# The last 128 tokens' second product in two halves of 256 columns, the second stored from ScalarE's queue

## The chip, the cores and the metric

One core of one Trainium2 chip. The metric is the device time of one execution of the program in microseconds; the median of three runs is compared. A profiled execution gives the span from the first to the last instruction and, for every engine, what it ran, what it waited for and which transfers it started.

## The reference

Eight batches of eight heads, 576 positions, head size 64. Attention looks back over a window of 64 positions; its output, laid out as 4608 tokens of 512 values, goes through two products with a hard-swish between them:

```python
scores = scale * np.matmul(q, k.transpose(0, 1, 3, 2))
mask = (rel >= 0) & (rel < window)
scores = np.where(mask, scores, -1000000000.0)
attn = softmax(scores)                       # written out in the reference
x = np.matmul(attn, v).transpose(0, 2, 1, 3).reshape(B * S, H * D)   # 4608 x 512
h = x @ w_in                                 # 512 -> 2048
g = h * np.clip(h + 3.0, 0.0, 6.0) / 6.0
out = (g @ w_out).astype(np.float32)         # 2048 -> 512
```

## The kernel before

Everything is written out by hand; no scheduler moves an instruction. An attention part makes the tokens, transposed, into `xT`. The two products run over nine blocks of 512 tokens. For each block, `first_units` (line 495) gives 16 units, one for each 128 of the 2048 hidden values: four matmuls into a bank `hT` (line 513), ScalarE's ReLU (line 525), VectorE's product (line 526) into `gT`. `second_units` (line 534) gives 16 more: four for each of the block's four groups of 128 tokens (`ts`), each unit with four matmuls of 128x512 (line 550), so that 16 of them sum up one bank `acc`. Behind the fourth unit of a group, ScalarE copies the bank into `osb` (line 556) and SP issues its store of 256 KB to `out` (line 558). `osb` comes from a pool of three buffers, `acc` of the last group of the last block from the pool `ps_t` of three banks.

The units stand in a list, `moe`, that the attention part draws from (`weave`, line 600) while it goes on. `queue_block` (line 567) puts a block's first units and second units of the block before into it. At the end, `queue_last` (line 581) appends block 7's remaining second units among block 8's first units, and then block 8's second units, four groups in order. So the last thing that TensorE does is the 16 matmuls of block 8's group `ts` = 3, and the last things at all are their copy and their store.

Ahead of that, `flagged` (line 605) tests whether all sums of the softmax were in range, each engine loads the flag (line 936), and behind the last unit stands a branch (line 938): if the flag is clear, `general` computes everything again in a safe way. Here it never is, so every engine jumps over the code of the fallback, which on each engine stands between the last unit and the program's end. Behind the jump each engine waits for its own instructions, SP also for the counters of all hardware DMA queues, eight of them (both under line 938); then SP reads further counters and the engines meet at GpSimd, which clears the semaphores (line 965).

ScalarE issues no DMA in this kernel: stores and SBUF-to-SBUF copies and transposes are issued by SP, loads by GpSimd.

Of the kernel before, what the change touches and what calls it, by code (L numbers as in the profile page):

```python
# [10 lines left out]
F32 = mybir.dt.float32  # L11
# [14 lines left out]
P = 128  # L26
# [11 lines left out]
def kernel(  # L38
# [9 lines left out]
    nc = tc.nc  # L48
    B, H, S, _ = q.shape
    DM, FF = moe_w_in.shape  # L50
# [5 lines left out]
    NFC = FF // P  # L56
    TB = 512
    XR = 6 * TB
    NTB = NT // TB
# [9 lines left out]
    osbp = ctx.enter_context(tc.tile_pool(name="osb", bufs=3))  # L69
    ps_o = ctx.enter_context(tc.tile_pool(name="ps_o", bufs=1, space=PSUM))  # L70
    ps_t = ctx.enter_context(tc.tile_pool(name="ps_t", bufs=3, space=PSUM))
# [11 lines left out]
    wout16 = consts.tile([P, NFC, DM], BF16, name="wout16")  # L83
# [409 lines left out]
    halfway, units, firsts = {}, {}, {}  # L493
# [40 lines left out]
    def second_units(kb):  # L534
        gT = gTs[kb]
        units, both = [], []
        for ts in range(TB // P):
            state = {}

            def unit(i, ts=ts, state=state):  # L540
                if i == 0 and late[0] == 0 and ts in (1, 2):
                    if ts == 1:
                        both.append(ps_o.tile([P, 2, 512], F32, name="acco", tag="o"))
                    state["acc"] = both[0][:, ts - 1]
                elif i == 0:
                    pool = ps_t if ts == 1 or late[0] == 2 and ts == 3 else ps_acc
                    state["acc"] = pool.tile([P, DM], F32, name="acc", tag="bk")[:]
                acc = state["acc"]
                for fc in range(4 * i, 4 * i + 4):
                    nc.tensor.matmul(  # L550
                        acc, lhsT=gT[:, fc, ts * P : (ts + 1) * P], rhs=wout16[:, fc, :],
                        start=(fc == 0), stop=(fc == NFC - 1),
                    )
                if i == NFC // 4 - 1:
                    osb = osbp.tile([P, DM], F32, name="osb")
                    nc.scalar.copy(out=osb[:], in_=acc)  # L556
                    u0 = kb * TB + ts * P
                    nc.sync.dma_start(out=out[u0 : u0 + P, :], in_=osb[:])

            units += [lambda i=i, unit=unit: unit(i) for i in range(NFC // 4)]  # L560
        return units

    moe = deque()
# [3 lines left out]
    def queue_block(kb, kept=2 * NG, lead=2):  # L567

        f = first_units(kb)
        moe.extend(left[:lead])  # L570
        del left[:lead]
        n = len(left)
        for i, unit in enumerate(f):
            moe.extend(left[i * n // NFC : (i + 1) * n // NFC])
            moe.append(unit)
        left[:] = second_units(kb)
        n = len(left) - kept
        moe.extend(left[:n])
        del left[:n]
# [109 lines left out]
    def warm(pool, n, cols=TB):  # L689
# [12 lines left out]
        out=ident[:], in_=ident[:], pattern=[[-1, P]], compare_op=mybir.AluOpType.not_equal,  # L702
# [115 lines left out]
    n = NG  # L818
# [151 lines left out]
```

## Time and profile before

| | us |
|---|---|
| runs | 315.24, 315.67, 315.19; median 315.24 |
| profiled execution | 316.28 |
| its span, first to last instruction | 314.6 |
| TensorE busy | 299.5 (95%) |
| ScalarE busy | 184.6 (59%) |
| VectorE busy | 180.4 (57%) |
| GpSimd busy | 131.3 (42%) |
| last copy of `acc` | 308.45 to 309.03 |

In the profile PE is TensorE's matmuls, PEld its weight loads, ACT ScalarE, DVE VectorE, POOL GpSimd and SP SyncE; an engine's name with a q (SPq, ACTq, PEldq) stands for its queue of issuing, branch and semaphore instructions, which aren't counted as busy. A row of a source line gives the count, the shortest, median and longest duration in ns, and the first and last start in us from the span's start. Timeline rows give start, length, and what ran. Groups give busy us and mean ns of one behind the bar, then the idle time before them and what ended it. "DMA to landing" is the time from a store's issue until its semaphore has its full count.

### The profile page before, as it was taken

The page shows a single profiled execution, that of the slowest core. Times are in us where ns is not written, and L with a number is a line of the kernel's source. Part 1 is how long each engine was busy: PE and PEld are TensorE (multiplying, and loading weights), DVE is VectorE, ACT ScalarE, POOL GpSimd, SP SyncE. Part 2 cuts the span into 40 slices and gives each one's busy share as a digit, 9 for nine tenths or more (in the row PEclk, how much of TensorE's full clock was granted, in tenths as well). Part 3 has the DMA queues.
Part 4 walks back from the last instruction along what each step waited for, and adds up shares of the span by engine and source line. Part 5 has one row for each costly group of instructions (what it writes and reads, how often), then busy time and mean ns, then how long its engine had stood idle before and what let it go on. Part 6 is the DMA issues. An engine that isn't in the chain of part 4 may idle for free.

```text
span 314.6 us, 10707 instructions
## 1 busy us (share of the span) xinstructions
PE 299.5 (95%) x4565; PEld 151.0 (48%) x4608; DVE 180.4 (57%) x411; ACT 184.6 (59%) x350; POOL 131.3 (42%) x181
## 2 busy tenths in 40 slices
PE   7889989999999999999999999999999999999992
PEld 3454445555555554444555555555544444444440
DVE  7767647598547755773577447754776155344200
ACT  3838555877658656773677457754764266454410
POOL 8861404868887536653665366533330000000000
PEclk9999999999999999999999999999999999999998
DMA  8999995969996976697469744983021100100121
GB/s 155 167 205 200 198 192 123 220 119 100 205 144 102 144 167 114 76 132 188 84 83 139 169 109 79 131 193 88 19 56 52 69 33 0 70 34 33 36 82 60
DMA packets 57848, 35.96 MB, mean 114 GB/s; under 512 B 40128, under 2 KB 51904, under 8 KB 57792
## 3 DMA queue, kind: packets, MB, share of 16 engines
q0 software_dynamic: 35744, 18.52, 45.8%
q1 hardware_dynamic: 22048, 16.67, 21.0%
q8 instruction: 38, 0.62, 0.8%
q14 instruction: 18, 0.15, 0.1%
HBM read 37.62 MB, written 9.44 MB: 150 GB/s over the span
## 4 chain that ended last, share of the span: by engine, by line
PE 81%; DMA 9%; POOL 3%; DVE 3%; issue 2%; ACT 1%; POOLq 0%; ACTq 0%; DVEq 0%
PE acc L550 36%; PE hT L513 34%; DMA qk<-in_q_dram 7%; PE o L421 4%; PE s L323 3%; DMA V<-in_v_dram 2%; PE tk L289 2%; PE acco L550 1%; POOL qk L117 1%; PE tq L289 1%; DVE gT L526 1%; POOL qk L128 1%; POOL wout L179 1%; DVE opl L448 0%; DVE V L160 0%
## 5 line engine op out<-in xcount | busy, mean ns | idle before, releaser
L526 DVE SCALAR_TENSOR_TENSOR gT<-t,hT 128x512 bf16<-128x512 bf16 x141 | 95.7, 686 | 74.3 <-ACT t L525 73.2
L513 PE MATMUL hT<-xT,win 128*128 128x512 bf16 x548 | 131.5, 379 | 1.1 <-DVE gT L526 0.2
L550 PE MATMUL acc<-wout,gT 128*128 128x512 bf16 x522 | 126.7, 379 | 2.5 <-issue 1.1
L525 ACT ACTIVATE t<-hT,half_const 128x512 bf16<-128x512 f32 x141 | 95.6, 689 | 48.2 <-PE hT L513 46.3
L513 PEld LDWEIGHTS <-win 128*128 128x128 bf16 x576 | 55.3, 98 | 65.2 <-issue 0.4
L550 PEld LDWEIGHTS <-gT 128*128 128x128 bf16 x576 | 54.5, 98 | 64.2 <-issue 0.9
L344 POOL TENSOR_TENSOR Pz<-e,band 128x512 bf16<-128x512 bf16 x48 | 54.1, 1144 | 0.0
L341 POOL TENSOR_TENSOR P<-e,first 64x256 bf16<-64x256 bf16 x24 | 15.8, 660 | 74.4 <-ACT e L332 74.4
L556 ACT COPY osb<-acc 128x512 f32<-128x512 f32 x34 | 19.9, 586 | 42.0 <-PE acc L550 42.0
L336 ACT ACTIVATE e<-s 128x512 bf16<-128x512 f32 x56 | 30.1, 591 | 0.0
L296 DVE COPY KT<-tk 128x576 bf16<-128x576 bf16 x28 | 21.0, 749 | 6.9 <-ACT e L332 5.8
L147 POOL DMA_DIRECT2D V<-in_v_dram x22 | 18.0, 829 | 8.5 <-DMA wout<-in_moe_w_out_dram 5.6
L448 DVE TENSOR_TENSOR opl<-o,recs 128x256 bf16<-128x256 f32 x52 | 19.6, 419 | 0.5
L430 DVE TENSOR_REDUCE sums<-o 128x10 f32<-128x20 f32 x26 | 4.6, 175 | 23.9 <-PE o L421 23.8
L296 ACT COPY QT<-tq 128x576 bf16<-128x576 bf16 x27 | 17.2, 638 | 1.5 <-PE tq L289 1.5
L332 ACT ACTIVATE e<-tk 64x128 bf16<-64x128 f32 x28 | 7.6, 270 | 17.7 <-PE tq L309 17.7
L421 PEld LDWEIGHTS <-Pz 64*64 64x64 bf16 x1008 | 11.4, 108 | 10.7 <-issue 10.2
L289 PE MATMUL tk<-ident,qk 64*64 64x64 bf16 x504 | 14.3, 195 | 0.0
L289 PE MATMUL tq<-ident,qk 64*64 64x64 bf16 x504 | 14.0, 195 | 0.3 <-DMA qk<-in_q_dram 0.3
L128 POOL DMA_DIRECT2D qk<-in_k_dram x22 | 14.1, 640 | 0.3 <-issue 0.3
L323 PE MATMUL s<-QT,KT 64*64 64x64 bf16 x896 | 13.8, 194 | 0.0
L128 POOL DMA_DIRECT2D qk<-in_q_dram x22 | 13.8, 627 | 0.0
(106 smaller groups left out, 199.9 us busy)
## 6 DMA issues: line engine op xcount, KB each, us to landing
out_dram<-osb SPq DMA_DIRECT2D x36, 256.0 KB, 2.5
V<-in_v_dram POOLq DMA_DIRECT2D x16, 256.0 KB, 6.0
qk<-in_q_dram POOLq DMA_DIRECT2D x19, 144.0 KB, 4.5
qk<-in_k_dram POOLq DMA_DIRECT2D x19, 144.0 KB, 4.3
V<-V SPq DMA_DIRECT2D x6, 432.0 KB, 5.1
wout<-in_moe_w_out_dram POOLq DMA_DIRECT2D x2, 1024.0 KB, 17.4
qk<-in_k_dram POOLq DMA_DIRECT2D x6, 288.0 KB, 4.4
qk<-in_q_dram POOLq DMA_DIRECT2D x6, 288.0 KB, 5.6
```

The lines of the kernel that those rows point to most:

```text
L128: nc.gpsimd.dma_start(out=t[halves[z], hs], in_=src[b, hs].rearrange("h (p r) d -> p h (r d)", r=RL))
L289: nc.tensor.transpose(out=hosts[t][z][halves[h], r * W : (r + 1) * W], in_=staged[b][halves[z], 2 * g + h, r * D : (r + 1) * D], identity= ...
L296: (nc.scalar.copy if z and not on_vector else nc.vector.tensor_copy)(out=(QT[t % 4][:] if z else KT[t % 4][:, W:]).rearrange("q (p r) -> q ...
L323: nc.tensor.matmul(ss[h][halves[i], c, m, r], lhsT=keys(t, h, W * (w - 1), r), rhs=QT[t % 4][halves[h], w * W : (w + 1) * W], start=True, ...
L336: nc.scalar.activation(out=e[:].rearrange("p c m r w -> p (c m r w)"), in_=ss[h][:].rearrange("p c m r w -> p (c m r w)"), func=EXP, scale ...
L344: muls[h].tensor_tensor(out=Pw[t % 4][:, h].rearrange("p c m r w -> p (c m) (r w)"), in0=e[:].rearrange("p c m r w -> p (c m) (r w)"), in1 ...
L421: nc.tensor.matmul(o[i][halves[c], c0 : c0 + D + 1], lhsT=p, rhs=vt[:, hh, v0 : v0 + D + 1], start=(r == 0), stop=(r == 1), skip_group_che ...
L513: nc.tensor.matmul(hT, lhsT=win16[:, g, fc * P : (fc + 1) * P], rhs=xT[:, g, t0 : t0 + TB], start=(g == 0), stop=(g == NG - 1),)
L525: nc.scalar.activation(out=t1[:], in_=hT, func=RELU, bias=half_const[:], scale=1.0 / 6.0)
L526: nc.vector.scalar_tensor_tensor(out=gT[:, fc, :], in0=t1[:], scalar=1.0, in1=hT, op0=MIN, op1=MULT)
L550: nc.tensor.matmul(acc, lhsT=gT[:, fc, ts * P : (ts + 1) * P], rhs=wout16[:, fc, :], start=(fc == 0), stop=(fc == NFC - 1),)
L556: nc.scalar.copy(out=osb[:], in_=acc)
```

## The change

In the last group of the last block (`kb` = 8, `ts` = 3), and in the same group of the fallback, the units are replaced by `half_unit`. The first two units make columns 0 to 255 with eight matmuls of 128x256 each, the last two columns 256 to 511. Each half has a bank of `ps_t`, a copy by ScalarE into a buffer of the same three `osb` buffers, and a store of 128 KB. The first half's store is issued by SP, the second half's by ScalarE. The `tag` only keeps the two shapes in one pool of three. The counters that SP waits for behind the jump are the same eight; ScalarE's store counts in one of them.

```diff
-                    osb = osbp.tile([P, DM], F32, name="osb")
+                    osb = osbp.tile([P, DM], F32, name="osb", tag="osb")
                     nc.scalar.copy(out=osb[:], in_=acc)
                     u0 = kb * TB + ts * P
                     nc.sync.dma_start(out=out[u0 : u0 + P, :], in_=osb[:])
 
-            units += [lambda i=i, unit=unit: unit(i) for i in range(NFC // 4)]
+            def half_unit(i, ts=ts, state=state):
+
+                j, part = divmod(i, 2)
+                n = DM // 2
+                cols = slice(j * n, (j + 1) * n)
+                if part == 0:
+                    state[j] = ps_t.tile([P, n], F32, name="acc", tag="bk")
+                for fc in range(8 * part, 8 * part + 8):
+                    nc.tensor.matmul(
+                        state[j][:], lhsT=gT[:, fc, ts * P : (ts + 1) * P], rhs=wout16[:, fc, cols],
+                        start=(fc == 0), stop=(fc == NFC - 1),
+                    )
+                if part:
+                    osb = osbp.tile([P, n], F32, name="osbh", tag="osb")
+                    nc.scalar.copy(out=osb[:], in_=state[j][:])
+                    u0 = kb * TB + ts * P
+                    (nc.scalar if j else nc.sync).dma_start(out=out[u0 : u0 + P, cols], in_=osb[:])
+
+            last = kb == NTB - 1 and ts == TB // P - 1
+            units += [lambda i=i, unit=half_unit if last else unit: unit(i) for i in range(NFC // 4)]
         return units
```

## The prediction

> **What bounds the kernel now.** I read the page first, then the timeline of the last 20 us, then the rows of the branch and closing lines.
>
> ```profile
> span 314.6 us, 10707 instructions
> ...
> PE 299.5 (95%) x4565; PEld 151.0 (48%) x4608; DVE 180.4 (57%) x411; ACT 184.6 (59%) x350; POOL 131.3 (42%) x181
> ...
> PE 81%; DMA 9%; POOL 3%; DVE 3%; issue 2%; ACT 1%; POOLq 0%; ACTq 0%; DVEq 0%
> ```
>
> TensorE is busy for 95% of the span and carries 81% of the chain that ended last. The change makes it no freer: it multiplies the same columns. What it can shorten is the stretch behind TensorE's last matmul, so I read that from the timeline.
>
> ```profile
> 294.18 13.70 PEld L550 LDWEIGHTS <-gT 128*128 128x128 bf16 x64
> 294.39 13.98 PE L550 MATMUL acc<-wout,gT 128*128 128x512 bf16 x63
> ...
> 305.61 3.79 SPq L558 DMA_DIRECT2D out_dram<-osb  x2
> 308.45 0.58 ACT L556 COPY osb<-acc 128x512 f32<-128x512 f32 x1 [2.87 <-PE acc L550]
> ```
>
> The last 64 matmuls (one record is missing; the weight loads count 64) run without a break to 308.4. ScalarE's copy takes 308.45 to 309.03, and SP issues the store until 305.61 + 3.79 = 309.40. The span ends at 314.6, so 6.2 us lie behind the last matmul. Who uses them? First the store's time to land, then the lines of the If and of the program's end.
>
> ```profile
> L558 SPq DMA_DIRECT2D out_dram<-osb x1: 333/333/333, 309.1 to 309.1; - x1
> ...
> DMA to landing us min/median/max: 2.6/2.6/2.6
> ```
>
> ```profile
> L938 SPq EVENT_SEMAPHORE  x8: 17/17/17, 312.3 to 312.9; - x8
> ...
> L938 DVEq COMPARE_BRANCH  x1: 72/72/72, 295.3 to 295.3; - x1
> L938 DVEq EVENT_SEMAPHORE  x1: 21/21/21, 298.4 to 298.4; - x1
> L938 PEldq COMPARE_BRANCH  x1: 3658/3658/3658, 304.3 to 304.3; - x1
> ...
> L938 ACTq COMPARE_BRANCH  x1: 50/50/50, 308.5 to 308.5; - x1
> L938 SPq COMPARE_BRANCH  x1: 58/58/58, 309.4 to 309.4; - x1
> L938 ACTq EVENT_SEMAPHORE  x1: 17/17/17, 311.2 to 311.2; - x1
> ...
> SPq L938 <- SPq L938: 2.8, 1, 2.8
> ```
>
> The store lands at 309.1 + 2.6 = 311.7. SP runs its branch over the fallback at 309.4 and its next instruction only at 312.3: 2.9 us, and the waits view names nothing but SP itself for 2.8 of them. That the store isn't the cause is shown by the other engines: ScalarE goes from branch (308.5) to next instruction (311.2) in 2.7 us, before the store has landed; VectorE in 3.1 (295.3 to 298.4), with no store of its own; TensorE's branch takes 3.66. Each engine pays about 3 us when it jumps. A transfer of instructions stands in SP's gap:
>
> ```profile
> q14 instruction: 1, 0.01, 5.7%
> ```
>
> This is the DMA view of 311.8 to 312.3, just ahead of SP's first instruction, 312.3. I read the gap as the wait for the code at the jump's target.
>
> ```profile
> L965 SPq DRAIN  x3: 7/7/12, 313.7 to 314.0; - x3
> L965 POOLq EVENT_SEMAPHORE  x4: 17/17/17, 313.8 to 314.5; - x4
> L965 ACTq DRAIN  x2: 8/8/8, 311.3 to 314.0; - x2
> ```
>
> SP reads eight DMA semaphores (312.3 to 312.9), more until 313.7; then GpSimd collects the engines at 313.8, and the end follows 0.8 later. ScalarE was done at 311.3. So the chain behind the last matmul is copy, SP's issue, **SP's jump**, SP's list, the joint end. The store's landing has slack: the list has passed all eight semaphores at 312.9, and the store was home at 311.7.
>
> **The change part by part.** TensorE's order up to the last 16 matmuls is the same. These 16 become 32 of 256 columns, with 16 more weight loads. No row has a 128x256 matmul; the nearest on both sides are 512 columns (above) and 128:
>
> ```profile
> 21.95 0.44 PE L392 MATMUL xp<-ident,opg 128*128 128x128 bf16 x5
> ...
> L392 PE MATMUL xp<-ident,opg 128*128 128x128 bf16 x20 | 1.9, 220 | 0.5 <-ACT xT L396 0.3 <-DVE opg L379 0.2
> ...
> L392 PEld LDWEIGHTS <-opg 128*128 128x128 bf16 x20 | 1.4, 97 | 1.7 <-DVE opg L379 1.1 <-issue 0.2
> ...
> L550 PE MATMUL acc<-wout,gT 128*128 128x512 bf16 x522 | 126.7, 379 | 2.5 <-issue 1.1 <-DMA wout<-in_moe_w_out_dram 0.6
> ```
>
> Start to start: (13.98 - 0.38) / 63 = 0.216 us at 512 columns, (0.44 - 0.22) / 4 = 0.055 at 128. On that line 256 columns take 0.055 + (0.216 - 0.055) / 3 = 0.109, and one alone 0.22 + 0.16 / 3 = 0.27. The weight loads (0.097) stay hidden even behind the 0.055 steps, so I add nothing for the 16 more; unhidden, they cost up to 0.098 a pair (a rival, below). The slice took 15 x 0.216 + 0.38 = 3.62; now 31 x 0.109 + 0.27 = 3.65, **0.03 later**. The first half is ready after 15 x 0.109 + 0.27 = 1.91, which is 1.71 earlier than the whole was. The halves take two banks of the pool, so TensorE doesn't wait for the first copy; its cover is the second half's 1.7 us, and without it the second half would start 0.4 late.
>
> ScalarE: one 128x512 copy (0.58) goes, two of 128x256 come. No such row; the nearest are
>
> ```profile
> L274 ACT ACTIVATE Pl<-sl 128x128 bf16<-128x128 f32 x4 | 1.1, 285 | 0.0
> ...
> L556 ACT COPY osb<-acc 128x512 f32<-128x512 f32 x34 | 19.9, 586 | 42.0 <-PE acc L550 42.0
> ```
>
> On the line between: 0.285 + 0.301 / 3 = 0.385, ends 0.285 and 0.586. First copy 308.45 - 1.71 = 306.74 to 307.12; it lies beside TensorE. Second copy 308.48 to **308.87**, 0.16 earlier than before.
>
> SP: its last store is now the first half's, issued at 307.15 to 307.48 (0.03 behind the copy and 0.33, as before). Nothing is queued behind it on SP but the branch, so SP jumps at 307.5 and is back at 307.5 + 2.9 = 310.4, **1.9 earlier**. That is the gain, and more than the halved copy gives. On its list it now also waits for ScalarE's store: it gets through the eight by 310.4 + 0.6 = 311.0 at the earliest.
>
> ScalarE's store: ScalarE issues no DMA in this trace, so the price is bounded by nothing and GpSimd's dearest issue; SP's rows are the nearest:
>
> ```profile
> L558 SPq DMA_DIRECT2D out_dram<-osb x36: 332/343/544, 43.7 to 309.1; - x36
> ...
> L179 POOL DMA_DIRECT2D wout<-in_moe_w_out_dram x2 | 1.8, 910 | 0.0
> ...
> DMA to landing us min/median/max: 2.0/2.1/2.6
> ```
>
> I take 0.33 (ends 0 and 0.91): 308.90 to 309.23. What is queued behind it on ScalarE is the branch, which before ran beside the copy (308.5) and now comes at 309.27: its jump ends at 309.27 + 2.7 = 312.0, and ScalarE is done 0.1 later, at **312.1** (before 311.3). ScalarE gets late where SP gets early. If its jump takes VectorE's 3.1, it is 312.5; TensorE's 3.66, 313.0.
>
> The second half's landing: the six stores of the last 28 us land 2.0 to 2.6 after issue (last row). With half the bytes I keep 2.0 to 2.6: 310.9 to 311.5. SP then finishes the eight at 311.0 to 311.6 and reaches its DRAIN 0.8 later (312.9 to 313.7 before): 311.8 to 312.4.
>
> TensorE's jump: it was taken 308.4 - 304.3 = 4.1 us ahead of TensorE's end, over queued matmuls. As many short instructions are 2.1 us, so the branch comes near 306.4 and ends at 310.0; even with no lead it would be 308.4 + 3.7 = 312.1. Not the last.
>
> Sum: GpSimd collects at the later of ScalarE (312.1) and SP (311.8 to 312.4), so 312.1 to 312.4; the end is 0.8 on, plus 0.05 to wake, 312.95 to 313.25. Against 314.6 that is 1.35 to 1.65 less; I take **1.55**. The profiled execution took 316.28, 1.7 more than its span; the median of the runs is 315.24. I carry the difference over: 315.24 - 1.55 = **313.7**. Own range: issue free and copies at 0.285 leave SP's 311.8 as the bound or a little less, 1.95 gained, 313.3; copy at 0.586, issue 0.54 and a jump of 3.1 add 0.2 + 0.2 + 0.4, 0.75 gained, 314.5.
>
> **The rivals.**
>
> *The landing sets the end.* Then SP's jump costs nothing of its own, and the end is 314.6 - 311.7 = 2.9 behind the landing: 310.9 to 311.5 gives 313.8 to 314.4, so 0.2 to 0.8 gained, 314.4 to 315.0. For it: SP comes back only 0.6 behind the landing. Against: ScalarE came back ahead of it. The Trainium skill, Advanced Engine Details and Errata, Control Flow Timing, gives a compare-and-branch as about 108 ns, which would make this the case; this trace disagrees where the branch is taken out of the code at hand (2.9 us). Chance 0.10.
>
> *ScalarE's own issue and jump eat the gain.* An issue of 0.91 and a jump of 3.66 add 0.58 + 0.96 = 1.5: 314.1 to 315.2. Against: its jump was 2.7. Chance 0.08.
>
> *A second store queue costs outside the span.* The 1.7 us there hold what is done for all queues; a tenth to all of it again gives 313.9 to 315.4. No row speaks for it. Chance 0.05.
>
> *The weight loads come into the open* (slower). Two loads where one was: under 256 columns (0.109) a load of 0.098 leaves 0.011. If every load has to wait for the matmul ahead of it, 32 x 0.098 = 3.1 us come on: 313.7 + 3.1 = 316.8; the change turns slower from 1.55 / 32 = 0.048 a pair. For it: the thin margin. Against: 0.055 steps with loads of 0.097. The Trainium skill, TensorE: Matmul & The Clock Gate, Part 3, The mechanism, says that a weight load overlaps matmuls in flight only if their row groups differ; here all are the same, and by that rule this rival holds. The 64 loads beside 0.216 steps disagree. Chance 0.07, with whatever else could be as dear.
>
> **How the numbers follow.** Forecast 0.70, all of it faster by over 0.2% (0.63 us, about what a measurement here can tell from no change: under 314.6). The landing: 0.04 faster, 0.06 same. ScalarE's price: 0.06 faster, 0.02 same. The queue: 0.03, 0.01 and 0.01 slower. Weight loads: 0.07 slower. Sums: faster 0.83, same 0.09, slower 0.08. The range 313.2 to 314.7 holds the forecast and the near ends of three rivals.
>
> **What would show it.** Right: SP's COMPARE_BRANCH near 307.5 and its next semaphore near 310.4; ScalarE's branch near 309.3, back near 312.0; first GpSimd collect at 312.1 to 312.4; span near 313.05. Wrong: 32 matmuls that take over 3.7 us; an issue on ScalarE over 0.6; SP back only at 312 or later although it jumped early; ScalarE's jump over 3.2; or a span that falls as told while the runs' median doesn't.

## The result and the profile after

The changed kernel takes 0.9957 of the time before, 95% interval 0.9941 to 0.9972: 1.36 us of 315.84 less (0.9 to 1.9). Over 22 runs each the medians are 314.42 and 315.84 us. The profiled execution took 313.15 us, its span is 311.4.

The spans differ by 3.2 us, more than the runs do, and that has to be taken apart first. The page of the changed kernel:

```profile
span 311.4 us, 10785 instructions
...
PE 303.2 (97%) x4624; PEld 152.4 (49%) x4624; DVE 180.7 (58%) x411; ACT 184.8 (59%) x351; POOL 131.4 (42%) x181
...
q10 hardware_dynamic: 144, 0.13, 0.1%
```

The weight loads (PEld) went from 4608 to 4624, 16 more, and so did the matmuls; the page before counts 4565 of them only because 43 records are missing, so the two busy times of PE can't be compared. q10 is a queue that the kernel before didn't have: ScalarE's store. To find where the spans part, I compared the times of the same instructions. VectorE's timeline of 56 to 62 us, first before, then changed:

```profile
60.85 0.69 DVE L526 SCALAR_TENSOR_TENSOR gT<-t,hT 128x512 bf16<-128x512 bf16 x1 [2.67 <-ACT t L525]
```

```profile
59.53 0.69 DVE L526 SCALAR_TENSOR_TENSOR gT<-t,hT 128x512 bf16<-128x512 bf16 x1 [2.67 <-ACT t L525]
```

1.3 us of the 3.2 are there by 61 us, in code that the change doesn't touch. In the other kernels of this study, which are the same up to there, this row lies between 59.5 and 62.0. In these two traces loads make the difference: between 29 and 60 us TensorE waits 0.6 us for a load of `wout` and 0.3 for one of `qk` before the change, and for neither in the changed kernel. The runs of the kernel before spread from 315.12 to 318.17. So one span against another says little here. I therefore measure a **closing stretch**: from the start of ScalarE's copy of group 2 (the same in all kernels, 128x512) to the span's end. The copy's row before:

```profile
304.99 0.58 ACT L556 COPY osb<-acc 128x512 f32<-128x512 f32 x1 [2.91 <-PE acc L550]
```

Before, the stretch is 314.6 - 304.99 = 9.6 us. The timeline of the changed kernel's end:

```profile
303.27 3.66 PE L568 MATMUL acc<-wout,gT 128*128 128x256 bf16 x32
303.51 0.58 ACT L556 COPY osb<-acc 128x512 f32<-128x512 f32 x1 [2.91 <-PE acc L550]
305.26 0.37 ACT L574 COPY osbh<-acc 128x256 f32<-128x256 f32 x1 [1.16 <-PE acc L568]
305.66 0.33 SPq L576 DMA_DIRECT2D out_dram<-osbh  x1
307.01 0.37 ACT L574 COPY osbh<-acc 128x256 f32<-128x256 f32 x1 [1.38 <-PE acc L568]
307.41 0.38 ACTq L576 DMA_DIRECT2D out_dram<-osbh  x1
```

Closing stretch: 311.4 - 303.51 = **7.9 us, 1.7 less**. The other 1.5 of the 3.2 lie ahead of it (304.99 - 303.51). The rows of the branch (line 957 here) and of the program's end (984) say where they went:

```profile
L957 SPq EVENT_SEMAPHORE  x8: 17/17/17, 308.7 to 309.3; - x8
...
L957 PEldq COMPARE_BRANCH  x1: 3598/3598/3598, 304.8 to 304.8; - x1
L957 SPq COMPARE_BRANCH  x1: 58/58/58, 306.0 to 306.0; - x1
L957 ACTq COMPARE_BRANCH  x1: 54/54/54, 307.8 to 307.8; - x1
L957 PEldq EVENT_SEMAPHORE  x1: 51/51/51, 308.5 to 308.5; - x1
L957 ACTq EVENT_SEMAPHORE  x1: 17/17/17, 310.4 to 310.4; - x1
```

```profile
L984 POOLq EVENT_SEMAPHORE  x4: 17/17/17, 310.6 to 311.3; - x4
L984 SPq DRAIN  x3: 7/7/13, 310.5 to 310.8; - x3
...
L984 ACTq DRAIN  x2: 8/8/8, 310.5 to 310.8; - x2
```

SP jumps 2.5 us behind group 2's copy (306.0 - 303.5; 4.4 before) and is back 2.7 later. ScalarE jumps at 4.3 and is back at 6.9, 2.6 later. ScalarE is now the last: SP, at the bottom of its list, waits for it, as the waits view of the changed kernel shows (total us, times, longest):

```profile
SPq L984 <- ACTq L957: 0.4, 1, 0.4
```

ScalarE's store landed 1.8 us after its issue, at 307.4 + 1.8 = 309.2: 1.2 ahead of ScalarE's return, but only 0.1 ahead of the end of SP's list of eight counters (309.3).

### The profile page after: what moved, and what is told of

It is laid out like the page before. It is cut to its first block, busy times and chain, and to the rows that moved or that the text cites. A ratio compares the mean times of both kernels' runs of the same rounds, so it can differ in the third digit from the quotient of the medians.

```text
span 311.4 us, 10785 instructions
## 1 busy us (share of the span) xinstructions
PE 303.2 (97%) x4624; PEld 152.4 (49%) x4624; DVE 180.7 (58%) x411; ACT 184.8 (59%) x351; POOL 131.4 (42%) x181
## 4 chain that ended last, share of the span: by engine, by line
PE 94%; DVE 3%; ACT 1%; issue 0%; ACTq 0%
PE hT L513 39%; PE acc L550 37%; PE o L421 4%; PE s L323 3%; PE acco L550 2%; PE tk L289 2%; PE wt L712 2%; PE acc L568 1%; PE tq L289 1%; PE hTo L513 1%; PE tp L223 1%; DVE gT L526 1%; DVE V L160 1%; DVE KT L243 0%; DVE opl L448 0%; PE xp L392 0%
## 5 line engine op out<-in xcount | busy, mean ns | idle before, releaser
L550 PEld LDWEIGHTS <-gT 128*128 128x128 bf16 x560 | 52.9, 98 | 61.6
L296 ACT COPY QT<-tq 128x576 bf16<-128x576 bf16 x27 | 17.2, 638 | 1.5 <-PE tq L289 1.5
L421 PEld LDWEIGHTS <-Pz 64*64 64x64 bf16 x1008 | 11.3, 108 | 10.6 <-issue 10.2
```

Of the source, the lines that this page charges most:

```text
L296: (nc.scalar.copy if z and not on_vector else nc.vector.tensor_copy)(out=(QT[t % 4][:] if z else KT[t % 4][:, W:]).rearrange("q (p r) -> q ...
L421: nc.tensor.matmul(o[i][halves[c], c0 : c0 + D + 1], lhsT=p, rhs=vt[:, hh, v0 : v0 + D + 1], start=(r == 0), stop=(r == 1), skip_group_che ...
L550: nc.tensor.matmul(acc, lhsT=gT[:, fc, ts * P : (ts + 1) * P], rhs=wout16[:, fc, :], start=(fc == 0), stop=(fc == NFC - 1),)
```

## The experiments

The theory is the prediction's: an engine pays some 3 us when it jumps over the fallback, and the end is set by the engine that comes last through its jump and its closing list. The main rival is that the landing of the last store, or its size, sets the end. Ratios are to the kernel before on the same chip. Each closing stretch comes from one profiled execution. Between these traces SP's jump took 2.6 to 3.0 us and ScalarE's 2.4 to 3.1, so a few tenths between two stretches show nothing unless the rows say where they come from.

| run | ratio (95% interval) | closing stretch, us |
|---|---|---|
| before | 1 | 9.6 |
| changed | 0.9957 (0.9941 to 0.9972) | 7.9 |
| both_sp | 0.9979 (0.9958 to 0.9999) | 9.4 |
| whole_act | 0.9950 (0.9929 to 0.9971) | 8.3 |
| nofb_before | 0.9927 (0.9901 to 0.9952) | 7.2 |
| nofb_after | 0.9908 (0.9885 to 0.9932) | 6.6 |
| uneven | 0.9937 (0.9916 to 0.9958) | 8.4 |
| pool_second | 1.0051 (1.0024 to 1.0078) | 10.6 |
| swap | 0.9995 (0.9981 to 1.0009) | 9.2 |
| both_act | 0.9943 (0.9922 to 0.9964) | 7.9 |
| early_if | 1.0024 (1.0004 to 1.0044) | 6.6, behind a pause of 2.8 |
| early_held | 0.9891 (0.9865 to 0.9918) | 6.8 |
| early_whole | 0.9910 (0.9881 to 0.9939) | 7.2 |

**Both halves stored by SP.**

```diff
-                    (nc.scalar if j else nc.sync).dma_start(out=out[u0 : u0 + P, cols], in_=osb[:])
+                    nc.sync.dma_start(out=out[u0 : u0 + P, cols], in_=osb[:])
```

> Both halves' stores are issued by SP. Measure: the closing stretch, from the start of the copy of group 2 (the last full 128x512 copy in the changed kernel, the last but one before) to the span's end; 9.6 us before, 7.9 changed. Theory (SP's jump over the fallback and its list come behind its last issue): SP issues last at 3.9 and jumps at 4.3, so the end comes at 9.3 to 9.4, some 0.2 less than before: time within 0.2% of before. Rival (it is the smaller, earlier stores that bring the gain): 7.9 to 8.1, time as the changed kernel's, 0.4% faster than before.

The closing stretch is 313.4 - 303.98 = 9.4. The rows of the branch:

```profile
L957 SPq EVENT_SEMAPHORE  x8: 17/17/17, 311.2 to 311.7; - x8
...
L957 SPq COMPARE_BRANCH  x1: 58/58/58, 308.3 to 308.3; - x1
```

SP jumps at 308.3, 4.3 behind the copy, and is back 2.9 later, as before the change. Two halves, two copies and two small stores bring 0.2 us together; who issues the last one brings the rest. By the runs alone this kernel can't be told from the changed one, as the two intervals overlap; swap, below, can be.

**The whole group stored by ScalarE.** The other half of the change alone.

```diff
-                    nc.sync.dma_start(out=out[u0 : u0 + P, :], in_=osb[:])
+                    last = kb == NTB - 1 and ts == TB // P - 1
+                    (nc.scalar if last else nc.sync).dma_start(out=out[u0 : u0 + P, :], in_=osb[:])
```

> No halves: the last group is made whole as before, but ScalarE issues its 256 KB store. Closing stretch 9.6 us before, 7.9 changed. Theory (what counts is which engine jumps last): SP jumps behind group 2's store; ScalarE issues from 4.1 to 4.45, is back from its jump at 7.1 to 7.2; the store lands at 6.1 to 6.7; end at 8.1 to 8.5, so 1.1 to 1.5 less than before, most of the change's gain without halves. Rival (the halves bring it): 9.6, no gain.

315.2 - 306.86 = 8.3: a gain of 1.3 of the change's 1.7, without halves. ScalarE's two rows:

```profile
L939 ACTq COMPARE_BRANCH  x1: 54/54/54, 311.3 to 311.3; - x1
L939 ACTq EVENT_SEMAPHORE  x1: 17/17/17, 314.2 to 314.2; - x1
```

It jumps at 4.4 and is back at 7.3; this jump took 2.9 against 2.6 in the changed kernel, so of the 0.4 to 0.5 between the two kernels only 0.2 is the shorter copy. The landing stands close behind the jump here: SP's list of eight ends only at 313.4, when ScalarE's store is home (issue 310.9, landing 2.3), and SP then waits 0.2 for ScalarE.

**Without the fallback, before and changed.** The body of the fallback is left out; on these inputs it never runs.

```diff
     with tc.If(safe < 1):
-        general()
+        nc.gpsimd.memset(seen[:], 0.0)
```

> The kernel before with the fallback's body left out (one memset of one element in its place; the fallback is never run on these inputs). Theory (the jump needs code that isn't at hand): with nothing to jump over the branch costs well under 0.5 us on SP and ScalarE, the store's landing sets the end: closing stretch 7.3 to 7.9 instead of 9.6, time 0.5 to 0.7% lower. Rival (the landing set the end before already): 9.4 to 9.6, less only by the eight semaphores that are not read.

> The changed kernel with the fallback's body left out in the same way. Theory: closing stretch 6.9 to 7.3, so halves and second queue gain 0.3 to 0.7 over the kernel without fallback and whole store (copy 0.2, a landing of 1.8 to 2.2 instead of 2.0 to 2.6), against 1.7 with the fallback. Rival (landing and halves are the gain): the same 1.4 to 1.7 between the two kernels without fallback.

312.9 - 305.71 = 7.2 and 311.4 - 304.76 = 6.6. The first is 2.4 us under the kernel before, with its whole store on SP. SP's rows there, from the views of the branch's line and of the end's:

```profile
L938 SPq COMPARE_BRANCH  x1: 58/58/58, 310.2 to 310.2; - x1
```

```profile
L965 SPq EVENT_SEMAPHORE  x14: 17/28/28, 310.4 to 312.8; - x14
```

From the branch to SP's next instruction it is 0.2 us instead of 2.9: same branch, same store, nothing to jump over. Now the landing sets the end: behind the branch SP waits 0.9 us for its store. The edit takes SP's list of eight counters away too, 0.6 us before; so at least 1.8 of the 2.4 are the jump's. Both kernels came out under the expected ranges. In nofb_before the store landed at 311.8 (issue 309.8, landing 2.0) and the end came 1.1 later; for nofb_after the profile gives no landing, so what made it shorter isn't shown. Between the two, halves and second queue are worth 0.5 to 0.6 us, a third of what they are worth with a fallback.

**Split at column 384.** The last copy and store become smaller still.

```diff
-                n = DM // 2
-                cols = slice(j * n, (j + 1) * n)
+                n = (3 * DM // 4, DM // 4)[j]
+                cols = slice(j * 3 * DM // 4, j * 3 * DM // 4 + n)
```

> The changed kernel split at column 384 instead of 256: the second part, stored by ScalarE, is half as large. Theory (jumps and SP's list): ScalarE's part gets 0.1 us earlier, but SP's last issue comes at 3.1 behind group 2's copy instead of 2.14, so SP jumps 1 us later than in the changed kernel, is back at 6.2 and through its lists at 7.5: the end moves from 7.84 to 8.2 to 8.4, slower than the changed kernel by 0.4 to 0.5 though its last copy and store are smaller. Rival (the size of what comes last sets the end): 7.7.

312.5 - 304.08 = 8.4, as the theory has it. The timeline and the branch's rows:

```profile
306.68 0.48 ACT L574 COPY osbh<-acc 128x384 f32<-128x384 f32 x1 [2.01 <-PE acc L568]
307.18 0.33 SPq L576 DMA_DIRECT2D out_dram<-osbh  x1
307.57 0.27 ACT L574 COPY osbh<-acc 128x128 f32<-128x128 f32 x1 [0.41 <-PE acc L568]
```

```profile
L957 SPq EVENT_SEMAPHORE  x8: 17/17/17, 310.2 to 310.8; - x8
...
L957 SPq COMPARE_BRANCH  x1: 58/58/58, 307.6 to 307.6; - x1
...
L957 ACTq EVENT_SEMAPHORE  x1: 17/17/17, 310.8 to 310.8; - x1
```

The larger first part makes SP's issue, and so its jump, 1.0 later than in the changed kernel (3.5 behind the copy instead of 2.5). ScalarE is back at 310.8, when SP still has its second list ahead, so SP is the last again. The runs don't show this: their median points the other way (0.9937 against 0.9957), with overlapping intervals. The two are told apart by the profile alone.

**The second half stored by GpSimd.**

```diff
-                    (nc.scalar if j else nc.sync).dma_start(out=out[u0 : u0 + P, cols], in_=osb[:])
+                    (nc.gpsimd if j else nc.sync).dma_start(out=out[u0 : u0 + P, cols], in_=osb[:])
```

> The changed kernel with the second half's store issued by GpSimd, whose jump took 0.2 us in the kernel before (251.5 to 251.7). SP and ScalarE then both jump early (SP back at 5.2 behind group 2's copy, ScalarE at 6.2). Theory: GpSimd issues from 3.9 to 4.75, its store lands at 6.5 to 7, it collects at 6.8 to 7.3, closing stretch 7.6 to 8.2, within 0.3 of the changed kernel's 7.84. Rival (GpSimd's own closing instructions are dear: its DRAIN took 2.4 us before): 9 or more.

A miss: 316.2 - 305.64 = 10.6, slower than before, which was the rival's case. From the views of GpSimd's issue, of the branch and of the end:

```profile
309.80 0.63 POOL L576 DMA_DIRECT2D out_dram<-osbh  x1 [74.36 <-ACT osbh L574]
```

```profile
L957 POOLq COMPARE_BRANCH  x1: 54/54/54, 309.8 to 309.8; - x1
...
L957 POOLq INC_SWDGE_SEM  x1: 787/787/787, 312.1 to 312.1; - x1
```

```profile
L984 POOLq DRAIN  x3: 46/107/2512, 312.9 to 316.0; - x3
```

GpSimd's jump takes only 0.2 us (309.8 to 310.0), but it then waits for its store until 312.1 and adds 0.8 for a semaphore update and a DRAIN of 2.5. In the kernel before these ran at 252 us, unseen.

**ScalarE first, SP second.**

```diff
-                    (nc.scalar if j else nc.sync).dma_start(out=out[u0 : u0 + P, cols], in_=osb[:])
+                    (nc.sync if j else nc.scalar).dma_start(out=out[u0 : u0 + P, cols], in_=osb[:])
```

> The changed kernel with the two issuers exchanged: ScalarE issues the first half's store, SP the second's. Same products, copies, sizes and number of queues. Theory (the engine with the longer closing work must issue early): SP issues last at 3.9 behind the start of group 2's copy, jumps at 4.3, and the closing stretch is 9.4 to 9.5 as with both on SP; ScalarE's early issue saves nothing. Rival (two queues side by side bring the gain): 7.8.

312.7 - 303.48 = 9.2, and the time is that of the kernel before. The stretch is 0.2 under what was expected: SP jumped at 4.2 behind the copy, not 4.3, and its jump took 2.8, not 2.9. Two queues bring next to nothing if SP is the one that issues last. SP's rows:

```profile
L957 SPq EVENT_SEMAPHORE  x8: 17/17/17, 310.5 to 311.0; - x8
...
L957 SPq COMPARE_BRANCH  x1: 58/58/58, 307.7 to 307.7; - x1
```

**Both halves stored by ScalarE.**

```diff
-                    (nc.scalar if j else nc.sync).dma_start(out=out[u0 : u0 + P, cols], in_=osb[:])
+                    nc.scalar.dma_start(out=out[u0 : u0 + P, cols], in_=osb[:])
```

> The changed kernel with both halves' stores issued by ScalarE; SP's last issue is then group 2's store, so SP jumps at 1.0 behind the start of group 2's copy instead of 2.5. Theory: SP isn't what ends last in the changed kernel, so nothing is gained: ScalarE jumps at 4.3 as before, closing stretch 7.8 to 8.2 (its jump took 2.6 to 2.9 so far). Rival (SP's list is the bound): 1.5 less, 6.4 to 7.0.

313.0 - 305.07 = 7.9, the changed kernel's. SP jumps 1.5 us earlier still and gains nothing by it: its list of eight waits until 310.8 for ScalarE's second store (issue 308.9, landing 1.8), and then SP waits 0.5 for ScalarE itself. The branch's row and the waits view:

```profile
L957 SPq EVENT_SEMAPHORE  x8: 17/17/17, 308.9 to 310.8; - x8
```

```profile
SPq L984 <- ACTq L957: 0.5, 1, 0.5
```

**The branch ahead of the last two groups.** If jumps are what costs, they belong beside TensorE's work.

```diff
-    weave(len(moe))
+    weave(len(moe) - 8)
+    behind_if = list(moe)
+    moe.clear()
     with tc.If(safe < 1):
         general()
+    for unit in behind_if:
+        unit()
...
-        gT = gpool.tile([P, NFC, TB], BF16, name="gT", tag="gT")
+        gT = gL if kb == NTB - 1 else gpool.tile([P, NFC, TB], BF16, name="gT", tag="gT")
```

`gL` is a buffer of its own for block 8; the fallback fills it too and leaves the last eight units out.

> The changed kernel with the branch and the fallback moved ahead of the last two groups of block 8, whose middle product gets a buffer of its own, so that both ways meet again before these groups: the jumps lie beside TensorE's queued matmuls. Measure: from the start of VectorE's last product to the span's end; 19.3 us before, 17.5 changed, 16.4 for the changed kernel without fallback. Theory: no jump is left at the end, the second half's landing sets it as without fallback, and TensorE pays a pause where the ways meet, 0.3 to 0.6: 16.7 to 17.1; 2.2 to 2.6 less than before, 0.7 to 0.8% faster than before. Rival (TensorE's jump of 3.6 us isn't hidden by its queue): a pause of 3 us or more, 19 to 20.

A miss, and not by the rival's reason. From the start of VectorE's last product the end comes 313.7 - 294.43 = 19.3 later, as before. The closing stretch is 6.6, so the jumps are gone from the end. But TensorE stands still at the meeting (its waits from 295 us on, and its timeline):

```profile
PE acc L551 <- ACTq L961: 2.8, 1, 2.8
```

```profile
303.37 3.61 PE L551 MATMUL acc<-wout,gL 128*128 128x512 bf16 x16 [2.78 <-ACTq L961]
```

TensorE's own jump was hidden (296.6 to 300.2, TensorE at work until 300.6). What it waited for is ScalarE. By the code, the next bank is one that ScalarE reads in the fallback too, so TensorE has to wait until ScalarE has come past the fallback, and ScalarE jumps only behind its copy of group 1 (300.6 to 303.3).

**The same with the sums of groups 0 and 1 held.**

```diff
+                elif i == 0 and kb == NTB - 1 and ts < 2:
+                    state["acc"] = held[0][:, ts]
...
+    held.append(ps_o.tile([P, 2, 512], F32, name="acch", tag="o"))
     queue_last(NTB - 2)
...
     with tc.If(safe < 1):
         general()
+    for ts in range(2):
+        kept[ts]()
```

`kept` holds the copy and store of these groups. The fallback keeps off the two banks (its `pv` takes others) and makes the two sums there again.

> The branch moved ahead again, now between groups 1 and 2 of block 8, but the sums of groups 0 and 1 stay in two banks that the fallback doesn't use (it makes these two sums again in the same banks), and are copied behind the place where the ways meet. ScalarE's and VectorE's last work ahead of the branch is then the product's last unit, 6.9 us ahead of TensorE's last matmul there, so their jumps (about 3 us) are over before TensorE needs them. Measure as for the first such kernel: from the start of VectorE's last product to the span's end; 19.3 before, 17.5 changed, 19.3 with the first one, where TensorE waited 2.8 us for ScalarE's jump. Theory: a pause of 0.3 to 0.6 is left where TensorE drains, 16.7 to 17.1, 0.4 to 0.8 less than the changed kernel; time 0.6 to 0.8% under before. Rival (the meeting itself costs TensorE its pause): 19 again.

311.5 - 294.67 = 16.8, as expected. TensorE's restart and the branch's rows:

```profile
301.10 3.61 PE L553 MATMUL acc<-wout,gL 128*128 128x512 bf16 x16 [0.28 <-PEq L971]
```

```profile
L971 ACTq COMPARE_BRANCH  x1: 50/50/50, 294.0 to 294.0; - x1
L971 SPq COMPARE_BRANCH  x1: 58/58/58, 294.1 to 294.1; - x1
...
L971 PEldq COMPARE_BRANCH  x1: 4134/4134/4134, 296.8 to 296.8; - x1
L971 ACTq EVENT_SEMAPHORE  x1: 17/17/17, 297.1 to 297.1; - x1
...
L971 PEldq EVENT_SEMAPHORE  x1: 51/51/51, 301.0 to 301.0; - x1
```

ScalarE jumps at 294.0 and is back at 297.1, SP likewise, all under TensorE's matmuls; a pause of 0.28 is left. At 0.9891 (0.9865 to 0.9918) its interval lies below the changed kernel's (0.9941 to 0.9972), each against the kernel before on its own chip. So this version beats both and keeps the fallback. As before, these inputs don't run the fallback.

**And the change undone there.** As early_held, with the last group made whole and stored by SP:

```diff
-            units += [lambda i=i, unit=half_unit if last else unit: unit(i) for i in range(NFC // 4)]
+            units += [lambda i=i, unit=unit: unit(i) for i in range(NFC // 4)]
```

> The same kernel with the last group made whole and stored by SP, as before the change: the change undone where no jump is left at the end. Theory: the change is then worth what it was without fallback, 0.4 to 0.6 (copy 0.2, landing and issue 0.2 to 0.4): 17.1 to 17.7 by the same measure. Rival (the change's 1.7 doesn't come from the jumps): 18.4 to 18.8.

313.2 - 296.03 = 17.2: the change is worth 0.3 to 0.5 us here by the profile (16.8 against 17.2 by this measure, 6.8 against 7.2 by the closing stretch), too little for the runs, whose intervals overlap.

## Why the prediction was right

It forecast 313.7 us, 1.55 less than the 315.24 of the first runs; measured are 1.36 (0.9 to 1.9) by the runs and 1.7 in the closing stretch. Over 22 runs both medians came out higher, the kernel before's by 0.6. Step by step, times behind group 2's copy:

- *What bounds the end.* The reading that SP's gap is its jump, not the store, holds: 2.9 us with a fallback, 0.2 without (nofb_before). That each engine pays about 3 us was too wide: GpSimd's jump took 0.2 in the kernel before as well (251.5 to 251.7); no run here shows why. The figure of 108 ns for a compare-and-branch (the Trainium skill, Advanced Engine Details and Errata, Control Flow Timing) is near the 0.2 us of the short jump, branch to next instruction, and far from the long one. For that, the Trainium skill, Runtime: NRT & Kernel Launch, Instruction fetch mechanics, says that a taken branch whose target lies outside the code already fetched stalls for its transfer; the two kernels without a fallback agree. That the gap is such a transfer remains a reading of the trace; how far a jump may reach was not tried.
- *The matmuls.* 3.65 predicted, 3.66 measured for all 32. The 32 loads stayed hidden, against the rule of the Trainium skill, TensorE: Matmul & The Clock Gate, Part 3, The mechanism, by which a load overlaps matmuls in flight only where their row groups differ, and the slower rival falls with it. The margin held even for narrower ones: the last 16 matmuls of uneven, 128x128 with a load of 98 ns each, start between 306.4 and 307.3, some 0.06 apart.
- *The copies.* 0.385 predicted, 0.372 measured.
- *SP's jump.* Predicted from 2.5 to 5.4, measured 2.5 to 5.2.
- *TensorE's jump.* Predicted from 1.4 to 5.0, measured from 1.3 to 4.9 (304.8 and 3.6 us): not the last.
- *ScalarE's issue and jump.* The issue took 0.38, not 0.33. The jump began at 4.3 as predicted and ended at 6.9, not 7.0. The row of before (2.7) carried over; from run to run ScalarE's jump took 2.4 to 3.1.
- *The landing.* 2.0 to 2.6 was kept; it took 1.8. The slack was smaller than that sounds: 0.1 until SP's list would have waited, and 0.4 that SP then had ahead of ScalarE. By these rows a landing of 2.6 would have set the end some 0.3 later (an estimate). In both_sp and swap the last store landed as fast, in 1.7 and 1.8, and next to nothing was gained, so the fast landing isn't where the gain comes from.
- *Who is last.* ScalarE, with SP 0.4 ahead. The prediction had the two within 0.3 and took a value between; by ScalarE alone it would have said 1.65. That is most of the difference between 1.55 and the 1.7 of the closing stretch. The runs, with 0.9 to 1.9, don't decide between the two; that the steps came true is read from the trace.
- *Outside the span* nothing was added: 316.28 - 314.6 = 1.7 before and 313.15 - 311.4 = 1.75 with the second queue.

## What to carry to other kernels

Read the stretch behind the last matmul by the branch and closing rows, not by the busy engines: if a gap on an issuing engine begins at a branch and ends with the engine waiting for nothing but itself, a smaller store helps little (0.2 us here), but an earlier last issue on that engine does. Give the last store to the engine with the least left to do behind it, or, better, move the branch to where the matrix engine has work queued; then check what the first instructions behind the meeting wait for, since an engine that jumps late holds up the others. And where runs differ by more than the change, compare a stretch that starts at the same instruction in all kernels.

## What the runs showed of the hardware that had not been expected

- A store issued by GpSimd at the end costs 2.5 us of DRAIN and 0.8 of semaphore update behind its landing (pool_second), although GpSimd's jump itself takes 0.2 us.
- ScalarE's issue of a store took 0.34 to 0.39 us on a queue that the kernel hadn't used, against SP's 0.33. The first use of the queue cost at most 0.05 more: in both_act the first issue took 0.39 and the second 0.34.
- In the changed kernel the first half's 128 KB landed in 2.6 us, the second half's in 1.8. That goes with the half and not with the issuer: with the issuers exchanged (swap) it is 2.6 from ScalarE and 1.8 from SP, with both on SP 2.4 and 1.7, with both on ScalarE 2.7 and 1.8. In early_held, whose jumps lie elsewhere, both landed in 1.7, and no transfer of instructions ran beside the first half's store. Such transfers did run beside both stores of the changed kernel, though, so why only the first was slower stays open.
